# Pinning every engine's queue by the kernel's own list scheduler

## The chip, the cores and the metric

The kernel runs on one core of one Trainium2 chip. The metric is the device time of one execution in microseconds (us), lower is better; the median of several runs is compared. The core has five queues that work at the same time and each strictly in order: PE (TensorE, matmuls and their weight loads), DVE (VectorE), ACT (ScalarE), POOL (GpSimd) and SP, which here only issues DMA transfers. An instruction that must wait for data from another engine holds up everything behind it on its own queue.

## The reference

Three stages, one after the other, in fp32 accuracy:

```python
# 1. linear attention with a complex decay; B=2, H=8, S=768, D=48
S_re, S_im = a_t * (S_re, S_im) + (outer(k_t, v_t), 0)   # for every step t
y_t = q_t @ S_re
# 2. x is y as 1536 x 384;  w_in 384 x 2048, w_out 2048 x 384
x = softplus(x @ w_in) @ w_out
# 3. four experts;  w1 384 x 1024, w2 1024 x 384 each, p the normalised domain_probs
out = sum(p[:, e:e+1] * (relu(x @ w1[e]) @ w2[e]) for e in range(4))
```

## The kernel before, in words

The 768 steps of each of the two batch entries are cut into chunks of 128. Two chunks form a pair, so there are six pairs, n = 0 to 5, each with the chunks c = 0 and 1. For a pair, DVE and ACT turn the factors a into logarithm and angle (`t`, `im`, `re`), PE makes their running sums by a matmul with a triangle (`pf` for the angle, `pl` for the logarithm, L592), a row of carry goes from chunk to chunk by a small DMA (`rows`) and a POOL addition (L573), and DVE multiplies the results with q and k into `QK` (L664). PE then transposes `QK` (`tp`, L673; ACT copies it to `qT` and `kT`), multiplies it to `sp` (L682), DVE masks that to `A` (L683), and PE makes the chunk's output `yps` (L698) and its state `sps` (L709). ACT and DVE write the output as a high and a low half of fp32r into `X` (L720, L721).

The two feed-forward stages are cut into twelve steps k: k = 0, 1 and 6, 7 are the softplus layer of batch 0 and 1 in halves of the hidden width, the others are the experts. They run in this order:

```python
ORDER = (0, 1, 2, 3, 6, 7, 4, 5, 8, 9, 10, 11)
```

For a block of tokens and 128 hidden columns, a step does a first product `h` (L233, nine matmuls: three pieces of the depth by three products of high and low halves), an activation on ACT (`e`, L248 and L103; then DVE, L251), the split into `g` high and low (L276 and L277, or L286 and L287), and the second product `y` or `z` (L315). Step 0 works in blocks of 256 tokens, two chunks, so its first product needs `X` of both chunks of pair 0. The weights of the softplus layer come as 64-bit words (`rawA`, `rawB`); DVE joins the two words in three instructions (L70 to L72, to `fA`, `fB`), ACT and DVE split them (L182, L183), and SP writes the joined weights to DRAM for batch 1 (L201). The tile names are followed by step, weight piece and half.

All this is emitted from a list of events, each with a position; a stage spreads its units over a stretch of positions beside the feed-forward steps:

```python
def put(units, lo, hi):
    for i, u in enumerate(units):
        events.append((lo + (hi - lo) * i / len(units), len(events), u))
...
put(back(0), -7.9, -3.8)
...
put(back(1), -0.7, 6.3)
```

What is emitted in this order goes to the framework's own scheduler, which takes the order of emission as priority and decides, by its own durations, in which order each engine's queue stands. The kernel adds a few edges without a wait (`behind`), which only keep the loads of ACT's function tables and a pair of matmuls in place. At the end comes a test that the inputs are in the range for which this fast path holds; it doesn't matter here.

Of the kernel before, what the change touches and what calls it, by code (L numbers as in the profile page):

```python
# [10 lines left out]
F32R = mybir.dt.float32r  # L11
# [6 lines left out]
PSUM = bass.MemoryType.PSUM  # L18
ACT = mybir.EngineType.Activation
# [4 lines left out]
P = 128  # L24
# [30 lines left out]
TRIG = "trig_and_small"  # L55


def decode(nc, dst, raw, b_exp, pool):
    e = pool.tile([P, 768], I32, name="dec_e", bufs=1)
    hi_ = raw[:, :, 1]  # L60
    nc.vector.tensor_scalar(e, hi_, 20, 0x7FF, ALU.logical_shift_right, ALU.bitwise_and)
    nc.scalar.activation(e, e, AF.Relu, bias=b_exp, scale=float(2 ** 23))
    nc.vector.tensor_scalar(dst.bitcast(I32), hi_, 0x000FFFFF, 0x00100000, ALU.bitwise_and, ALU.bitwise_or)
    nc.vector.scalar_tensor_tensor(dst, raw[:, :, 0].bitcast(U32), 2.0 ** -32, dst.bitcast(I32), ALU.mult, ALU.add)
    nc.vector.scalar_tensor_tensor(e, hi_, -0x80000000, e, ALU.bitwise_and, ALU.bitwise_or)
    nc.vector.scalar_tensor_tensor(dst, dst, 2.0 ** -20, e.bitcast(F32), ALU.mult, ALU.mult)
# [9 lines left out]
def fast_path(ctx: ExitStack, tc, bad, wsc, qkv, a_re, a_im, w_in, w_out, probs, w1, w2, out):  # L76
    nc = tc.nc

    const = ctx.enter_context(tc.tile_pool(name="const", bufs=1))
    wp = ctx.enter_context(tc.tile_pool(name="wp", bufs=1))  # L80
    xa = ctx.enter_context(tc.tile_pool(name="xa", bufs=1))
    ac = ctx.enter_context(tc.tile_pool(name="ac", bufs=1))
    tmp = ctx.enter_context(tc.tile_pool(name="tmp", bufs=1))
    att_ctx = ExitStack()
    att = att_ctx.enter_context(tc.tile_pool(name="att", bufs=1))
    psum = ctx.enter_context(tc.tile_pool(name="psum", bufs=1, space=PSUM))
    early_ctx = ExitStack()
    early = early_ctx.enter_context(tc.tile_pool(name="early", bufs=1, side="right"))

    NOSYNC = mybir.DependencyInfo(mybir.DependencyClass.NoSync, mybir.DependencyReason.DATA)  # L90
    tabs = {"load": None, "since": []}

    def behind(ins, earlier):
        tc.add_manual_dep(ins.ins, earlier.ins.name, NOSYNC, reason="order on one engine")

    def use_table(name):
        load = nc.scalar.preload_act_table_set(name)  # L97
        for i in tabs["since"]:
            behind(load, i)
        tabs["load"], tabs["since"] = load, []  # L100

    def act(out_, in_, fn, **kw):
        i = nc.scalar.activation(out_, in_, fn, **kw)  # L103
        if fn in (AF.Exp, AF.Ln, AF.Sin, AF.Arctan):
            behind(i, tabs["load"])
            tabs["since"].append(i)
        return i
# [7 lines left out]
                            base=0, channel_multiplier=-1)  # L115
# [150 lines left out]
    def second(k, blk, f):  # L266
        if k % 6 >= 2:
            return
        key = (k, blk, f)
        if k == 0:  # L270
            if f % 2 == 0:
                return
            t = t_t.pop(key)
            hi, lo = (tmp.tile([P, 2, WM], F32R, tag="g", name=f"g{i}{k}_{blk}_{f}", bufs=GB).rearrange("p a b -> p (a b)")[:, :512]
                      for i in range(2))
            nc.scalar.copy(hi, t)  # L276
            nc.vector.tensor_tensor(lo, t, hi.bitcast(F32), ALU.subtract)  # L277
            for i in range(2):
                g_t[k, blk, f - 1 + i] = [x[:, i * 256:(i + 1) * 256] for x in (hi, lo)]
            if f == 1:  # L280
                low_sum(k, blk, hi[:, :256], 256)
            return
        t = t_t.pop(key)
        TB = span(k, blk)[-1]
        g = tmp.tile([P, 2, WM], F32R, tag="g", name=f"g{k}_{blk}_{f}", bufs=GB)[:, :, :TB]
        (nc.scalar.copy if k == 1 else nc.vector.tensor_copy)(g[:, 0, :], t)  # L286
        nc.vector.tensor_tensor(g[:, 1, :], t, g[:, 0, :].bitcast(F32), ALU.subtract)  # L287
        g_t[key] = g
        if k == 6 and f == 0:
            low_sum(k, blk, g[:, 0, :], TB)  # L290

    def third(k, blk, f):
# [15 lines left out]
        for j in range(nj):  # L308
            for n, (p, q) in enumerate(((0, 0), (0, 1), (1, 0))):
                if s < 2:  # L310
                    l_, r_ = wt[:, q, f % 2, j * P:(j + 1) * P], g[p] if k == 0 else g[:, p, :]
                else:
                    l_, r_ = g[:, p, j * P:(j + 1) * P], wt[:, q, f % 2, :]
                mate = k == 0 and j == 1
                mm = nc.tensor.matmul(ys[j], l_, r_, start=(opens and n == 0 and not mate),  # L315
                                      stop=(closes and n == 2), skip_group_check=k == 0)
                if opens and n == 0:
                    if mate:
                        behind(mm, opened)
                    opened = mm  # L320
# [55 lines left out]
    late = {}  # L376
# [139 lines left out]
    def flush():  # L516
        if len(pipe) > 0:
            second(*pipe[-1])
        while pipe:
            third(*pipe.pop(0))  # L520
# [242 lines left out]
    def run():  # L763
        for _, _, u in sorted(events, key=lambda e: e[:2]):
            u()
        events.clear()
# [5 lines left out]
    one = [slice(0, 1), slice(1, 2)]  # L772
# [26 lines left out]
    base = [0] + [24 + 16 * i for i in range(12)]  # L799
    ring = []  # L800
# [11 lines left out]
    for m, k in enumerate(ORDER):  # L812
        if k in FAST:
# [6 lines left out]
            for i in range(16):  # L820
                hh, r = divmod(i, 8)
# [6 lines left out]
            for n in range(8):  # L828
                j = n // 2
                if n % 2 == 0:  # L830
                    need, last = base[m] + 4 * j, base[m] + 4 * j + 4
                else:
                    need = base[m] + 8 * (j // 2) + 4 + 2 * (j % 2)
# [20 lines left out]
    for pos, need, last, k, n in sorted(fast_events):  # L854
# [3 lines left out]
        for i, u in enumerate(us):  # L858
            at = pos if i == 0 else max(pos + 2.5, need - 5.2 + 1.7 * (i - 1))
# [8 lines left out]

    def swap():
        early_ctx.close()  # L870
        xb = ctx.enter_context(tc.tile_pool(name="xb", bufs=1, side="right"))
        XB[1] = xb.tile([P, 2, KT, S], F32R, name="X1")

    put([swap], base[2] + 3.5, base[2] + 4)
# [2 lines left out]
    w_ = (b1 - b0) / 3  # L877
    for i, n in enumerate((3, 4, 5)):
        at = b0 + i * w_
# [4 lines left out]

    def switch():
        att_ctx.close()
        lp = ctx.enter_context(tc.tile_pool(name="late", bufs=1))
        for n in "xugwh":
            late[n] = lp
        home[1] = lp  # L890
# [50 lines left out]
    put(checks + [verdict], base[8] + 2, base[12] - 2)  # L941
    run()
    flush()


@with_exitstack
def general_path(ctx: ExitStack, tc, xs, v, qkv, a_re, a_im, w_in, w_out, probs, w1, w2, out):
# [80 lines left out]
    for t, src in zip(ws, (w_in, w_out)):  # L1028
        for j in range(8):
            raw = wk.tile([P, 768, 2], I32, name="graw", bufs=1)  # L1030
            nc.sync.dma_start(raw.rearrange("p a w -> p (a w)"), src.bitcast(I32)[j])
            decode(nc, t[:, j, :], raw, b_exp, wk)
# [65 lines left out]
@with_exitstack  # L1098
def attention_moe_kernel(ctx: ExitStack, tc, qkv, a_re, a_im, w_in, w_out, probs, w1, w2, v, out):
    nc = tc.nc  # L1100
    top = ctx.enter_context(tc.tile_pool(name="top", bufs=1))
    bad = top.tile([1, 1], I32, name="bad")
    wsc = nc.dram_tensor("moe1_weights", (16, P, 768), F32).ap()
    fast_path(tc, bad, wsc, qkv, a_re, a_im, w_in, w_out, probs, w1, w2, out)
    xs = nc.dram_tensor("attention_out", (NTOK, HD), F32).ap()
    flag = nc.values_load(bad[0:1, 0:1], min_val=0, max_val=1)
    with tc.If(flag > 0):
        general_path(tc, xs, v, qkv, a_re, a_im, w_in, w_out, probs, w1, w2, out)
# [53 lines left out]
```

## Time and profile before

| | before |
|---|---|
| time, median of 3 runs | 736.75 us (736.65 to 739.24) |
| the profiled execution | 736.14 us, of which the span from first to last instruction is 734.4 us |
| PE busy, share of the span | 699.3 us, 95% |
| DVE busy | 580.3 us, 79% |
| ACT busy | 488.2 us, 66% |
| granted TensorE clock, mean | 0.989 of full speed |

A matmul's records overlap, so "busy" is the time covered by at least one of them, and a PE that is busy need not be at its full rate. The shares are means over stages that differ: attention and the joining of weights load DVE and ACT in the first 140 us, after that the feed-forward steps alone set the load of PE.

### The profile page before, as it was taken

The page shows a single profiled execution, that of the slowest core. Times are in us where ns is not written, and L with a number is a line of the kernel's source. Part 1 is how long each engine was busy: PE and PEld are TensorE (multiplying, and loading weights), DVE is VectorE, ACT ScalarE, POOL GpSimd, SP SyncE. Part 2 cuts the span into 40 slices and gives each one's busy share as a digit, 9 for nine tenths or more (in the row PEclk, how much of TensorE's full clock was granted, in tenths as well). Part 3 has the DMA queues.
Part 4 walks back from the last instruction along what each step waited for, and adds up shares of the span by engine and source line. Part 5 has one row for each costly group of instructions (what it writes and reads, how often), then busy time and mean ns, then how long its engine had stood idle before and what let it go on. Part 6 is the DMA issues. An engine that isn't in the chain of part 4 may idle for free.

```text
span 734.4 us, 13295 instructions
## 1 busy us (share of the span) xinstructions
PE 699.3 (95%) x5171; PEld 674.2 (92%) x5171; DVE 580.3 (79%) x1139; ACT 488.2 (66%) x898; POOL 29.5 (4%) x29
## 2 busy tenths in 40 slices
PE   2778999999999999999999999999999999999997
PEld 1567898999899999999999999999999999999997
DVE  6899998945774863648888789988888898988963
ACT  8887885878995856345676666564556566666640
POOL 0112010000112011000000000000000000000000
PEclk9799999999999999999999999999999999999999
DMA  8666665721221330121022030213445445454512
GB/s 268 193 200 194 214 188 188 225 65 44 68 62 60 103 100 2 58 87 44 23 85 67 23 100 29 87 44 87 138 151 150 142 147 176 151 172 135 171 40 69
DMA packets 36486, 83.56 MB, mean 114 GB/s; under 512 B 4544, under 2 KB 13376, under 8 KB 36416
## 3 DMA queue, kind: packets, MB, share of 16 engines
q1 hardware_dynamic: 36128, 82.35, 36.3%
q8 instruction: 42, 0.69, 0.4%
q10 hardware_dynamic: 288, 0.30, 0.1%
q14 instruction: 28, 0.23, 0.1%
HBM read 73.95 MB, written 8.65 MB: 112 GB/s over the span
## 4 chain that ended last, share of the span: by engine, by line
PE 71%; ACT 12%; DVE 8%; DMA 6%; issue 2%; POOL 0%; SPq 0%; DVEq 0%; ACTq 0%; POOLq 0%
PE y L315 21%; PE h L233 16%; PE z L315 10%; PE px L426 8%; PE pv L426 4%; PE pc L426 2%; PE yps L698 2%; PE tp L673 2%; PE sp L682 2%; DMA chkw<-in_w_in_dram 2%; ACT L97 2%; ACT t L103 1%; ACT e L103 1%; DMA rawB<-in_w_dram 1%; PE ya L360 1%
## 5 line engine op out<-in xcount | busy, mean ns | idle before, releaser
L233 PE MATMUL h<-X,A 128*128 128x384 f32 (+1 forms) x936 | 174.9, 328 | 1.6 <-DVE e L251 0.9
L233 PEld LDWEIGHTS h<-X,A 128*128 128x128 f32 x936 | 152.6, 189 | 5.0 <-issue 1.8
L315 PE MATMUL y<-B,g 128*128 128x384 f32 x744 | 150.2, 335 | 0.2 <-DVE acc L346 0.2
L315 PEld LDWEIGHTS y<-B,g 128*128 128x128 f32 x744 | 131.1, 188 | 0.7 <-ACT he L446 0.5
L315 PE MATMUL y<-g,B 128*128 128x384 f32 (+1 forms) x504 | 90.3, 315 | 0.9 <-ACT g L286 0.3
L315 PE MATMUL z<-B,g 128*128 128x384 f32 x372 | 84.8, 335 | 0.0
L315 PEld LDWEIGHTS y<-g,B 128*128 128x128 f32 x504 | 78.9, 189 | 2.0 <-ACT g L286 0.7
L315 PEld LDWEIGHTS z<-B,g 128*128 128x128 f32 x372 | 66.5, 188 | 0.0
L248 ACT ACTIVATE e<-h 128x384 f32<-128x384 f32 (+1 forms) x60 | 30.7, 511 | 34.5 <-PE h L233 30.5
L251 DVE SCALAR_TENSOR_TENSOR e<-h,e 128x384 f32<-128x384 f32 (+1 forms) x60 | 34.8, 580 | 20.1 <-ACT e L103 19.1
L256 DVE SCALAR_TENSOR_TENSOR g<-h,g 128x384 fp32r<-128x384 f32 x32 | 17.7, 553 | 28.2 <-ACT g L255 28.2
L103 ACT ACTIVATE e<-e,b_one 128x384 f32<-128x384 f32 (+1 forms) x60 | 38.2, 637 | 1.4
L673 PE MATMUL tp<-ident,QK 128*96 128x128 f32 x192 | 27.1, 288 | 8.2 <-DVE QK L664 7.8
L673 PEld LDWEIGHTS tp<-ident,QK 128*96 128x96 f32 x192 | 22.3, 132 | 12.8 <-issue 4.9
L103 ACT ACTIVATE e<-e 128x384 f32<-128x384 f32 (+1 forms) x60 | 32.8, 546 | 1.2
L426 PE MATMUL px<-XC,sA 128*128 128x384 f32 x144 | 33.1, 338 | 0.5 <-DVE ha L452 0.5
L426 PE MATMUL px<-X,sA 128*128 128x384 f32 x144 | 33.3, 337 | 0.0
L315 PE MATMUL z<-g,B 128*128 128x384 f32 x144 | 33.3, 337 | 0.0
L287 DVE TENSOR_TENSOR g<-e,g 128x384 fp32r<-128x384 f32 x48 | 26.6, 554 | 6.1 <-ACT g L286 5.5
L255 ACT ACTIVATE g<-h 128x384 fp32r<-128x384 f32 x32 | 15.7, 489 | 21.9 <-PE h L233 21.7
L491 ACT CAST B<-rawB 128x768 fp32r<-128x768 f32 x24 | 20.0, 834 | 13.2 <-DMA rawB<-in_w_dram 6.2
L491 ACT CAST A<-rawA 128x384 fp32r<-128x384 f32 (+1 forms) x48 | 20.3, 457 | 11.7 <-DMA rawA<-in_w_dram 9.4
(204 smaller groups left out, 1409.3 us busy)
## 6 DMA issues: line engine op xcount, KB each, us to landing
rawA<-in_w_dram SPq DMA_DIRECT2D x32, 384.0 KB, 3.1
rawB<-in_w_dram SPq DMA_DIRECT2D x32, 384.0 KB, 3.1
rawA<-in_w_in_dram SPq DMA_DIRECT2D x16, 384.0 KB, 3.5
rawB<-in_w_out_dram SPq DMA_DIRECT2D x16, 384.0 KB, 3.4
chkw<-in_w_in_dram SPq DMA_DIRECT2D x16, 384.0 KB, 3.4
chkw<-in_w_out_dram SPq DMA_DIRECT2D x16, 384.0 KB, 3.3
qk<-in_qkv_dram SPq DMA_DIRECT2D x12, 384.0 KB, 3.2
v<-in_qkv_dram SPq DMA_DIRECT2D x12, 256.0 KB, 3.2
```

The lines of the kernel that those rows point to most:

```text
L97: load = nc.scalar.preload_act_table_set(name)
L103: i = nc.scalar.activation(out_, in_, fn, **kw)
L233: nc.tensor.matmul(ps, wt[:, p, kk, o:o + P], XB[b][:, q, kk, tok], start=(n == 0), stop=(n == 3 * KT - 1))
L248: nc.scalar.activation(t, h, AF.Abs)
L251: nc.vector.scalar_tensor_tensor(t, h, 0.0, t, ALU.max, ALU.add)
L255: nc.scalar.activation(g[:, 0, :], h, AF.Relu)
L256: nc.vector.scalar_tensor_tensor(g[:, 1, :], h, 0.0, g[:, 0, :].bitcast(F32), ALU.max, ALU.subtract)
L287: nc.vector.tensor_tensor(g[:, 1, :], t, g[:, 0, :].bitcast(F32), ALU.subtract)
L315: mm = nc.tensor.matmul(ys[j], l_, r_, start=(opens and n == 0 and not mate), stop=(closes and n == 2), skip_group_check=k == 0)
L426: nc.tensor.matmul(ps, lt[:, p, li, :], rhs, start=(start and n == 0), stop=(stop and n == 2), skip_group_check=True)
L491: nc.scalar.copy(hi, src)
L673: nc.tensor.transpose(tp[:96, hh, :], src[:, hf * 4 + hh, :], ident)
```

## The change: what it does

All tile pools are wrapped in a class that notes for each tile its ring of buffers. When everything is emitted, `arrange` takes all instructions of the program, works out who needs whom (overlapping areas, free buffers), groups consecutive PE instructions that write one PSUM tile into one job that nothing may enter, and schedules all engines together: the engine that can start soonest takes, among its jobs that are ready by then, the one emitted first. Durations are a table in `cost`. Every queue is then pinned in the order found, by edges without waits (`behind` of each instruction on the one ahead of it). No computation is added or removed, the positions of the events stay, and the waits between engines stay those that the data need. All lines of the old code stand 241 further down in the new one (L233 becomes L474). The core of the diff:

```diff
+class Queues:
...
+    def behind(self, ins, earlier):
+        info = mybir.DependencyInfo(mybir.DependencyClass.NoSync, mybir.DependencyReason.DATA)
+        self.tc.add_manual_dep(ins, earlier.name, info, reason="order on one engine")
...
+    def cost(self, i, e, ins, outs):
...
+        if kind == "InstDMACopy":
+            return (0.45 if out * outs[0].ap[0][1] > 7500 else 0.1), 0.0
...
+            if i.ins[0].dtype == F32R:
+                hold = max(0.109, out * 0.4375e-3 + 0.005)
...
+        if e == DVE:
+            wide = [ap for ap in ins if math.prod(c for _, c in ap.ap[1:]) > 1]
+            fast = kind in ("InstTensorScalarPtr", "InstTensorCopy") and len(wide) == 1 and not self.in_psum(wide[0])
+            t = n / (1.92e3 if fast else 0.96e3)
+            return t + 0.07, t + 0.15
+        if e == ACT:
+            t = n / 0.96e3 + (0.1 if any(ap.tensor.name.startswith("b_") for ap in ins) else 0.0)
+            return t + 0.02, t + (0.075 if any(map(self.in_psum, ins)) else 0.11)
+        if e == POOL:
+            return (1.05, 1.1) if outs[0].ap[0][1] == 1 else (0.2 + n * 2.3e-3, 0.25 + n * 2.3e-3)
...
+    def arrange(self):
...
+            out = touch[k][1][0].tensor.name if eng[k] == PE and touch[k][1] else None
+            if out is None:
+                job[k] = len(jobs)
+                jobs.append([k])
+            else:
+                if prev is None or prev[0] != out:
+                    prev = (out, len(jobs))
+                    jobs.append([])
+                job[k] = prev[1]
+                jobs[prev[1]].append(k)
...
+        while any(ready):
+            best = None
+            for e in range(5):
+                if ready[e]:
+                    soon = max(free[e], min(ready[e].values()))
+                    j = min(j for j, t in ready[e].items() if t <= soon)
+                    if best is None or soon < best[0]:
+                        best = (soon, e, j)
+            _, e, j = best
+            del ready[e][j]
+            for k in jobs[j]:
+                t = start[k] = max(free[e], from_when(k))
+                hold, seen_ = cost[k]
...
+                    slow = 1.9 if e == PE and 15 < t < 36 else 1.0
+                    hold, seen_at[k] = hold * slow, t + seen_ * slow
+                free[e] = t + hold
+                queue[e].append(k)
...
+        for q in queue:
+            for a, b in zip(q, q[1:]):
+                self.behind(todo[b], todo[a])
...
-    const = ctx.enter_context(tc.tile_pool(name="const", bufs=1))
+    queues = Queues(tc)
+    const = queues.pool(ctx, "const")
...
     run()
     flush()
+    queues.arrange()
```

How this moves instructions is seen at three places. The first is DVE's queue ahead of the first product: the row L721 of `yps_1` writes the last `X` that the first `h` needs. Before, it stands here:

```order
66 L600 SCALAR_TENSOR_TENSOR im_132<-im_132,pf_1_367 128x384
67 L72 SCALAR_TENSOR_TENSOR fA_1_1_514<-rawA_1_1_500,fA_1_1_514 128x384
68 L183 TENSOR_TENSOR A_1_497<-fA_1_0_502,A_1_497 128x384
69 L683 TENSOR_TENSOR A_1_0_372<-sp_1_0_373,tri 128x512
70 L70 TENSOR_SCALAR fB_1_0_553<-rawB_1_0_535 128x384
71 L683 TENSOR_TENSOR A_1_1_386<-sp_1_1_387,tri 128x512
72 L554 TENSOR_TENSOR re_481<-re_481,t_483 128x768
73 L183 TENSOR_TENSOR A_1_497<-fA_1_1_514,A_1_497 128x384
74 L555 SCALAR_TENSOR_TENSOR re_481<-re_481,t_483 128x768
75 L71 SCALAR_TENSOR_TENSOR fB_1_0_553<-rawB_1_0_535,fB_1_0_553 128x384
76 L721 TENSOR_TENSOR X_121<-yps_1_393,X_121 128x3x128
77 L715 TENSOR_TENSOR S_317<-sps_1_436,S_317 96x512
```

In the changed kernel the same place of DVE's queue reads:

```order
75 L841 SCALAR_TENSOR_TENSOR im_132<-im_132,pf_1_367 128x384
76 L312 SCALAR_TENSOR_TENSOR fB_1_0_553<-rawB_1_0_535,fB_1_0_553 128x384
77 L311 SCALAR_TENSOR_TENSOR fB_1_1_574<-rawB_1_1_537,fB_1_1_574 128x384
78 L924 TENSOR_TENSOR A_1_0_372<-sp_1_0_373,tri 128x512
79 L312 SCALAR_TENSOR_TENSOR fB_1_1_574<-rawB_1_1_537,fB_1_1_574 128x384
80 L924 TENSOR_TENSOR A_1_1_386<-sp_1_1_387,tri 128x512
81 L424 TENSOR_TENSOR B_1_534<-fB_1_0_553,B_1_534 128x384
82 L310 TENSOR_SCALAR fA_2_0_631<-rawA_2_0_617 128x384
83 L956 TENSOR_TENSOR S_317<-sps_1_436,S_317 96x512
84 L311 SCALAR_TENSOR_TENSOR fA_2_0_631<-rawA_2_0_617,fA_2_0_631 128x384
85 L312 SCALAR_TENSOR_TENSOR fA_2_0_631<-rawA_2_0_617,fA_2_0_631 128x384
86 L962 TENSOR_TENSOR X_121<-yps_1_393,X_121 128x3x128
```

`X` of `yps_1` has moved from row 76 to row 86: ten instructions that stood behind it stand ahead of it now, eight of them the joining and splitting of weights, the others the state `S` (L715) and one of the factors of pair 2 (L556). Nothing that stood ahead of it has gone behind it.

The second place is DVE's queue in step 0, block 1, where L251 makes `e_1_3` from the product `h_1_2`. Before:

```order
165 L664 TENSOR_TENSOR QK_1_1302<-qk_1_769,im_482 128x16x48
166 L70 TENSOR_SCALAR fA_1_0_1365<-rawA_1_0_1324 128x384
167 L70 TENSOR_SCALAR fA_1_1_1409<-rawA_1_1_1326 128x384
168 L71 SCALAR_TENSOR_TENSOR fA_1_0_1365<-rawA_1_0_1324,fA_1_0_1365 128x384
169 L721 TENSOR_TENSOR X_121<-yps_0_1190,X_121 128x3x128
170 L72 SCALAR_TENSOR_TENSOR fA_1_0_1365<-rawA_1_0_1324,fA_1_0_1365 128x384
171 L71 SCALAR_TENSOR_TENSOR fA_1_1_1409<-rawA_1_1_1326,fA_1_1_1409 128x384
172 L554 TENSOR_TENSOR re_2146<-re_2146,t_2148 128x768
173 L251 SCALAR_TENSOR_TENSOR e_1_3_1232<-h_1_2_1152,e_1_3_1232 128x512
```

After the change DVE's queue reads there:

```order
164 L924 TENSOR_TENSOR A_0_1_1183<-sp_0_1_1184,tri 128x512
165 L505 TENSOR_SCALAR stats<-stats 128x1
166 L492 SCALAR_TENSOR_TENSOR e_1_3_1232<-h_1_2_1152,e_1_3_1232 128x512
167 L310 TENSOR_SCALAR fA_1_0_1365<-rawA_1_0_1324 128x384
168 L310 TENSOR_SCALAR fA_1_1_1409<-rawA_1_1_1326 128x384
169 L311 SCALAR_TENSOR_TENSOR fA_1_0_1365<-rawA_1_0_1324,fA_1_0_1365 128x384
170 L311 SCALAR_TENSOR_TENSOR fA_1_1_1409<-rawA_1_1_1326,fA_1_1_1409 128x384
171 L518 TENSOR_TENSOR g_1_3_1286<-e_1_3_1232,g_1_3_1285 128x512
172 L312 SCALAR_TENSOR_TENSOR fA_1_0_1365<-rawA_1_0_1324,fA_1_0_1365 128x384
173 L962 TENSOR_TENSOR X_121<-yps_0_1190,X_121 128x3x128
```

Here the move goes the other way: seven instructions that stood ahead of `e_1_3` now stand behind it.

The third place is SP's queue of DMA issues near the start, where `rows` is the carry and `rawB_0_1` a half of the first weights of the second product. Before:

```order
13 L193 DMA rawB_0_0_470<-in_w_out_dram 128x768
14 L618 DMA rows_1_205<-zl_130 1x16x24
15 L193 DMA rawB_0_1_472<-in_w_out_dram 128x768
16 L538 DMA re_481<-in_a_re_dram 128x2x384
17 L539 DMA im_482<-in_a_im_dram 128x2x384
18 L147 DMA pr<-in_probs_dram 128x48
19 L201 DMA moe_weights<-fA_0_0_379 128x384
```

After, SP's queue reads:

```order
13 L434 DMA rawB_0_0_470<-in_w_out_dram 128x768
14 L434 DMA rawB_0_1_472<-in_w_out_dram 128x768
15 L388 DMA pr<-in_probs_dram 128x48
16 L779 DMA re_481<-in_a_re_dram 128x2x384
17 L442 DMA moe_weights<-fA_0_0_379 128x384
18 L434 DMA rawA_1_0_498<-in_w_in_dram 128x768
19 L442 DMA moe_weights<-fA_0_1_426 128x384
```

The carry row L618 has left row 14; it stands at row 25 now, behind its sister row L617. From step 1 on (row 260 of DVE's queue and behind) the two kernels have nearly the same order on every engine; what differs there are neighbours that change places, and PE jobs that are no longer cut in two.

## Rows read from the trace of the kernel before

**Rows 1.** Windows: busy us (count) of PE, PEld, DVE, ACT, POOL; clock, DMA share, GB/s.

```profile
9.00:20.00 11.00, 5.33 (x9) 2.84 (x10) 10.81 (x19) 10.03 (x18) 0.00 (x0) 0.79 0.86 307
20.00:40.00 20.00, 15.85 (x139) 10.83 (x139) 17.93 (x33) 17.47 (x31) 4.87 (x4) 0.77 0.65 204
40.00:60.00 20.00, 14.68 (x198) 12.64 (x196) 19.39 (x34) 18.58 (x32) 2.23 (x2) 1.00 0.52 155
60.00:140.00 80.00, 76.07 (x906) 71.29 (x906) 75.91 (x146) 60.61 (x112) 7.73 (x4) 1.00 0.66 206
140.00:360.00 220.00, 218.89 (x1808) 210.70 (x1807) 140.87 (x234) 152.62 (x266) 13.58 (x11) 1.00 0.22 65
360.00:729.00 369.00, 368.19 (x2119) 365.77 (x2117) 312.49 (x663) 223.21 (x434) 0.00 (x0) 1.00 0.35 108
```

**Rows 2.** Waits of PE, 8.94 to 140 us: total us, times, longest.

```profile
PE tp L673 <- DVE QK L664: 7.5, 3, 3.8
PE pf L592 <- ACT im L103: 5.7, 1, 5.7
PE pf L592 <- POOL im L573: 2.3, 2, 1.4
PE h L233 <- DVE e L251: 0.9, 1, 0.9
```

**Rows 3.** Timeline of DVE, 38 to 49 us: start, length, instruction.

```profile
38.65 0.35 DVE L70 TENSOR_SCALAR fA<-rawA 128x384 int32<-128x384 int32 x1
38.92 0.67 DVE L713 COPY S<-sps 96x512 f32<-96x512 f32 x1
...
41.38 0.54 DVE L72 SCALAR_TENSOR_TENSOR fA<-rawA,fA 128x384 int32<-128x384 int32 x1
41.85 0.54 DVE L183 TENSOR_TENSOR A<-fA,A 128x384 fp32r<-128x384 f32 x1
...
46.47 0.57 DVE L721 TENSOR_TENSOR X<-yps,X 128x384 fp32r<-128x384 f32 x1
46.94 0.70 DVE L715 TENSOR_TENSOR S<-sps,S 96x512 f32<-96x512 f32 x1
47.54 0.97 DVE L556 TENSOR_TENSOR im<-im,re 128x768 f32<-128x768 f32 x1
48.40 0.57 DVE L72 SCALAR_TENSOR_TENSOR fB<-rawB,fB 128x384 int32<-128x384 int32 x1
```

**Rows 4.** Timeline of PE, 47 to 55 us and 86 to 88 us; idle before in brackets.

```profile
47.10 4.09 PE L233 MATMUL h<-X,A 128*128 128x256 f32 x32 [0.47 <-DVE X L721]
54.98 1.49 PE L673 MATMUL tp<-ident,QK 128*96 128x128 f32 x12 [3.79 <-DVE QK L664]
...
86.05 1.24 PE L315 MATMUL y<-g,B 128*128 128x256 f32 x9
87.13 1.24 PE L233 MATMUL h<-X,A 128*128 128x256 f32 x9
```

**Rows 5.** Timeline of DVE, 98 to 104 us.

```profile
98.80 0.62 DVE L70 TENSOR_SCALAR fA<-rawA 128x384 int32<-128x384 int32 x2
99.34 0.55 DVE L71 SCALAR_TENSOR_TENSOR fA<-rawA,fA 128x384 int32<-128x384 int32 x1
...
100.42 1.58 DVE L72 SCALAR_TENSOR_TENSOR fA<-rawA,fA 128x384 int32<-128x384 int32 x1
...
103.27 0.68 DVE L251 SCALAR_TENSOR_TENSOR e<-h,e 128x512 f32<-128x512 f32 x1
```

**Rows 6.** Timeline of POOL, 60 to 130 us.

```profile
63.51 2.59 POOL L548 TENSOR_TENSOR t<-t,t 128x768 f32<-128x768 f32 x1 [6.27 <-ACT t L547]
...
98.53 3.06 POOL L548 TENSOR_TENSOR t<-t,t 128x768 f32<-128x768 f32 x1 [24.43 <-ACT t L547]
```

**Rows 7.** Timeline of SP, the DMA queue, 13 to 25 us.

```profile
13.60 0.63 SPq L618 DMA_DIRECT2D rows<-zl  x1
14.27 0.56 SPq L193 DMA_DIRECT2D rawB<-in_w_out_dram  x1
...
24.57 0.51 SPq L617 DMA_DIRECT2D rows<-tail  x1
```

More of the change, by code (lines that the diff above doesn't have):

```diff
@@ L55, with __init__, tile @@
 TRIG = "trig_and_small"
+ENGINES = {mybir.EngineType.PE: 0, mybir.EngineType.DVE: 1, mybir.EngineType.Activation: 2,
+           mybir.EngineType.Pool: 3, mybir.EngineType.SP: 4}
+PE, DVE, ACT, POOL, SP = range(5)
+class Pool:
+    def __init__(self, queues, pool, name, after):
+        self.queues, self.pool, self.name, self.after = queues, pool, name, after
+    def tile(self, shape, dtype, tag=None, name=None, bufs=1):
+        t = self.pool.tile(shape, dtype, tag=tag or name, name=name, bufs=bufs)
+        self.queues.home[t.name] = ((self.name, tag or name), bufs, self.after)
+        return t
@@ L77, in fast_path @@
     nc = tc.nc
-    const = ctx.enter_context(tc.tile_pool(name="const", bufs=1))
[L80 to L83, printed above, removed]
+    queues = Queues(tc)
+    const = queues.pool(ctx, "const")
+    wp = queues.pool(ctx, "wp")
+    xa = queues.pool(ctx, "xa")
+    ac = queues.pool(ctx, "ac")
+    tmp = queues.pool(ctx, "tmp")
     att_ctx = ExitStack()
-    att = att_ctx.enter_context(tc.tile_pool(name="att", bufs=1))
-    psum = ctx.enter_context(tc.tile_pool(name="psum", bufs=1, space=PSUM))
+    att = queues.pool(att_ctx, "att")
+    psum = queues.pool(ctx, "psum", space=PSUM)
     early_ctx = ExitStack()
-    early = early_ctx.enter_context(tc.tile_pool(name="early", bufs=1, side="right"))
-    NOSYNC = mybir.DependencyInfo(mybir.DependencyClass.NoSync, mybir.DependencyReason.DATA)
+    early = queues.pool(early_ctx, "early", side="right")
     tabs = {"load": None, "since": []}
     def behind(ins, earlier):
-        tc.add_manual_dep(ins.ins, earlier.ins.name, NOSYNC, reason="order on one engine")
+        queues.behind(ins.ins, earlier.ins)
+        queues.order_only.append((ins.ins.name, earlier.ins.name))
     def use_table(name):
@@ L870, in swap @@
         early_ctx.close()
-        xb = ctx.enter_context(tc.tile_pool(name="xb", bufs=1, side="right"))
+        xb = queues.pool(ctx, "xb", after="early", side="right")
         XB[1] = xb.tile([P, 2, KT, S], F32R, name="X1")
@@ L886, in switch @@
         att_ctx.close()
-        lp = ctx.enter_context(tc.tile_pool(name="late", bufs=1))
+        lp = queues.pool(ctx, "late", after="att")
         for n in "xugwh":
```

154 lines of the change are left out of this document (added).

## The prediction

> **What bounds the kernel now.** I read the windows first, since a share over the whole span mixes stages. PE idles 5.67 us of the 11 between 9 and 20 us, 4.15 between 20 and 40, 5.32 between 40 and 60, 3.93 between 60 and 140, 1.11 between 140 and 360, and 0.81 from there to 729 [rows 1]. So from 140 us on PE is full, and no order of the queues can give more than 1.92 us there; what can be won lies in the 19.07 us before. DVE, in the same windows, idles 2.07 us between 20 and 40, 0.61 between 40 and 60 and 4.09 between 60 and 140: 6.77 us of 120, it is the busiest engine until 60 us and level with PE until 140 [rows 1]. The waits of PE name the same thing: 7.5 us for `QK` from DVE, 5.7 for the arctangent on ACT right after the start, 2.3 for the carry that POOL adds, 0.9 for `e` from DVE [rows 2]. The granted clock is 0.77 to 0.79 between 9 and 40 us, where PE has only gapped work, and 1.00 behind that [rows 1]; PE waits there for others, so a faster or slower clock in that stretch is not priced.
>
> The profiled execution took 736.14 us (span 734.4), 0.6 below the median of the runs, 736.75. I make the sum against the former and add 0.6 at the end.
>
> **The change, part by part.** No instruction comes or goes, and edges without waits cost nothing by themselves: each is between two neighbours of one queue, which run in that order anyway. So PE's work is fixed, and the time moves by what its idle time gains or loses.
>
> *9 to 40 us.* The first 5.67 us wait for the first arctangent on ACT, whose chain from the first loads keeps its order. On SP the carry `rows<-zl`, which waits until 13.60, no longer holds up the weights behind it, issued at 14.27 [rows 7]; they can go right behind the issue before. But what PE waits for in this stretch is `QK` and the carry (L617, issued at 24.57), not these weights. I take 0; ends: 0.9 gained (the carry's shorter wait, 2.3 less 1.4 [rows 2]) and 0.5 lost (one more weight step of 0.47 us ahead of the first `QK`).
>
> *40 to 60 us: a loss.* `X` of `yps_1` gets ten DVE instructions more ahead of it. Start to start they cost: a join or split step 0.47 us (41.38 to 41.85), L70 0.27 (38.65 to 38.92), L715 0.60 (46.94 to 47.54), L556 0.86 (47.54 to 48.40) [rows 3]. Six steps, two L70, one L715 and one L556 are 2.82 + 0.54 + 0.60 + 0.86 = 4.8 us. By that alone the first `h` starts at 51.9 instead of 47.10 [rows 4], and PE has nothing else to do. But before the change PE idles again right behind it, 3.79 us, until `QK` of pair 1 lets the transposes start at 54.98 [rows 4]. Most of the ten stand ahead of that `QK` already; new ahead of it are only one split, one L70 and two join steps, 1.7 us. So the delay that is left at the transposes is 1.7 us, less what DVE's own idle shrinks until there. Of the 2.68 us of DVE idle between 20 and 60 [rows 1] I take a third, 0.9, since the new order chooses among ready work but can't make data come sooner. Loss: 0.8 us. Ends: a gain of 1.0 (all of the 2.68 gone) and a loss of 4.8 (nothing absorbed).
>
> *60 to 140 us: a gain.* Here the order moves the other way. `e_1_3` (103.27) loses seven instructions ahead of it, which took from 98.80 to 103.27, 4.5 us [rows 5]; by the same count `e_1_7` of step 0 loses five steps and one L70, 2.6 us, and `e_1_5`, between the two, 1.2 us. These instructions are the ones that feed PE; what is put behind them is weights that are wanted later. PE's visible idle in this window is 3.93 us [rows 1], of it the 0.9 for `e` and 1.4 for POOL's carry [rows 2], which also starts from DVE. The earlier DVE work exceeds most of these waits, so I take four fifths: 3.1 us. Ends: 0 and 3.9.
>
> *Inside the busy time.* Nine matmuls of 256 columns take 1.08 us start to start at best (86.05 to 87.13), 0.120 each; the 32 at 47.10 took 4.09, 0.128 each [rows 4]. Step 0 has three blocks of eight pieces with nine matmuls each for `h` and `y`, 432 in all; at 0.008 us each the small waits that no gap shows are at most 3.5 us. Jobs that are not cut and inputs that come earlier may close a part; I take 0.8. Ends: 0 and 3.5.
>
> *POOL beside DVE.* The list of durations has no price for DVE and POOL at once. In the trace, L72 took 1.58 us at 100.42, under POOL's addition of 3.06 us that began at 98.53, instead of 0.55, so 1.0 us lost [rows 5, 6]. The order decides which DVE instruction meets POOL, not whether one does: 0. [...] By rows the ends are a gain of 1.0 and a loss of 4.6 (5.65 us of POOL's own length [rows 6], less 1.0).
>
> *140 us to the end.* The orders agree but for neighbours; of 1.92 us idle nothing is promised to go: 0. Ends: 1.9 gained; 1.0 lost, if a transposition now kept behind a whole `h` job makes a chain late by one such job of nine 0.120 us matmuls [rows 4].
>
> Sum: + 0.8 - 3.1 - 0.8 = - 3.1 us; 736.14 - 3.1 = 733.0, and 733.6 for the median, rounded to 733.5.
>
> **The rivals.**
>
> *A larger gain.* DVE loses nearly all its idle and PE's gaps behind 20 us close. Adding the good ends, 0.9 + 1.0 + 3.9 + 3.5 + 1.9 = 11.2 us, gives 725.5; a likely value is three quarters, 728. For it: only weight work is moved, and DVE is loaded to 94% (113.2 of 120 us [rows 1]), so cover is always there. Against: the first 5.67 us and most of the 7.5 for `QK` are chains through several engines.
>
> *No change.* The loss ahead of the first `h` is 1.7 us, with none of DVE's idle won back, and the 60 to 140 gain is half, 2.0: 736.4. For it: the old order was also made by emission order and readiness, and behind step 0 most rows agree.
>
> *Slower.* The first `X` is late by 4.8 us, and PE doesn't get it back, because the waits behind it are not DVE's load but chains that begin with this `X` or with PE itself. With nothing won the time is 736.75 + 4.8 = 741.5. It decides from the point where the transposes of pair 1 start later than 54.98 by more than the 3.93 us that can be had behind 60.
>
> [...]
>
> **How the numbers follow.** About 0.5%, 3.7 us, is what a measurement of this kernel can tell from no change. My forecast, 731.5 to 735.5, has 0.43, a little over half of it below the line at 733.1: 0.22 faster, 0.21 same. The larger gain has 0.24, all faster. No change has 0.17, the port 0.04, both same. Slower has 0.12; 0.11 of it lies beyond the line at 740.4, 0.01 within. Together: faster 0.46, same 0.43, slower 0.11. The range goes from 726, near the sum of the good ends, to 740, into the slower case; it leaves out some 0.13.
>
> **What would show it.** In the trace after: the first long run of `h` starts 3 to 5 us later than 47.10, and the transposes behind it at 55 to 57. PE's idle between 60 and 140 is under 1.5 us. DVE's idle between 20 and 140 is under 6 us. From 140 on PE is as full as before. I am wrong if the transposes come later than 58, if PE's idle behind 60 stays at 4 us although `e` comes earlier, or if gaps on PE open behind 140 us, where the pinned queues can't step aside for a late transfer.

## The result, and the profile after

The changed kernel takes 730.9 us, median of 5 runs (728.62 to 732.11), against 736.75: the ratio of the mean times is 0.9903, 95% interval 0.9875 to 0.9932, so 5.0 to 9.2 us less. The forecast was 733.5, range 726 to 740: faster, as forecast, by about twice as much. The profiled execution took 730.9 us, span 729.1. A few executions of 785 us and more, of changed and unchanged kernels alike, are left out of all ratios here.

The windows of the changed kernel, columns as in [rows 1]:

```profile
9.00:20.00 11.00, 4.93 (x8) 2.27 (x8) 10.80 (x19) 9.57 (x17) 0.00 (x0) 0.78 0.79 291
20.00:40.00 20.00, 13.67 (x132) 9.32 (x130) 19.79 (x38) 18.99 (x33) 4.04 (x3) 0.78 0.82 264
40.00:60.00 20.00, 17.58 (x197) 15.25 (x198) 17.58 (x27) 15.90 (x29) 5.19 (x4) 0.83 0.41 129
60.00:140.00 80.00, 77.93 (x937) 74.92 (x937) 75.69 (x148) 63.18 (x118) 6.59 (x4) 1.00 0.64 199
140.00:360.00 220.00, 219.43 (x1816) 213.48 (x1816) 144.73 (x241) 153.12 (x268) 13.36 (x11) 1.00 0.21 66
360.00:724.00 364.00, 363.34 (x2086) 360.09 (x2085) 305.99 (x655) 219.09 (x429) 0.00 (x0) 1.00 0.35 109
```

PE's idle is the stretch less the first busy number. It grew between 20 and 40 us from 4.15 to 6.33, and fell from 5.32 to 2.42 between 40 and 60, from 3.93 to 2.07 between 60 and 140, and from 1.11 to 0.57 between 140 and 360; behind that it is 0.66. The weight loads (second number) say more than that: between 60 and 140 us they cover 74.92 us instead of 71.29, with 937 matmuls instead of 906. PE does more in the same window than its busy time shows. The granted clock differs too: 0.83 between 40 and 60 us, where it was 1.00 before [rows 1].

The waits of PE up to 140 us, in the changed kernel:

```profile
PE pf L833 <- ACT im L344: 6.1, 1, 6.1
PE tp L914 <- DVE QK L905: 3.0, 1, 3.0
PE tp L914 <- ACT qT L915: 2.2, 1, 2.2
PE h L474 <- DVE e L492: 1.8, 1, 1.8
PE tp L914 <- ACT kT L915: 1.3, 1, 1.3
PE pl L833 <- POOL t L814: 1.0, 2, 0.8
```

Against [rows 2]: the waits for `QK` fell from 7.5 us to 3.0, those for POOL's carry from 2.3 to 1.0. The wait for `e` grew from 0.9 to 1.8. The transposes now wait 2.2 and 1.3 us for the copies `qT` and `kT` on ACT; before it was 0.2 for `qT`.

The timeline of PE at the first `h`, in the changed kernel, answers to [rows 4]:

```profile
43.01 1.65 PE L833 MATMUL pl<-t,tri 128*128 128x384 f32 x2 [0.75 <-POOL t L814]
44.45 3.62 PE L923 MATMUL sp<-qT,kT 96*128 96x128 f32 x16
...
52.10 0.50 PE L474 MATMUL h<-X,A 128*128 128x256 f32 x2 [0.61 <-ACT X L961]
52.96 4.33 PE L474 MATMUL h<-X,A 128*128 128x256 f32 x34 [0.36 <-DVE X L962]
57.13 1.91 PE L914 MATMUL tp<-ident,QK 128*96 128x128 f32 x16
```

The long run of `h` starts 5.9 us later than 47.10, but the transposes behind it only 2.15 later than 54.98, and with no wait. The product `sp` ahead of it was late already; in the kernel before it stands here:

```profile
40.45 2.29 PE L682 MATMUL sp<-qT,kT 96*128 96x128 f32 x16
```

Up to the transposes PE runs the same 312 matmuls in both kernels, and from there to the fifth `h` job of step 1 (at 148.05 and 143.98 us) again the same work, all but a few matmuls that overlap the edges. These stretches compare better than windows at fixed times; columns as in [rows 1], first the kernel before, then the changed one:

```profile
0.00:54.98 54.98, 31.68 (x312) 22.85 (x313) 45.59 (x88) 46.91 (x78) 7.20 (x13) 0.88 0.69 221
54.98:148.05 93.07, 88.02 (x984) 82.07 (x984) 88.19 (x168) 73.50 (x140) 8.72 (x5) 1.00 0.65 201
0.00:57.13 57.13, 34.33 (x312) 24.88 (x313) 48.19 (x93) 48.19 (x81) 9.18 (x14) 0.82 0.68 223
57.13:143.98 86.85, 84.78 (x986) 81.63 (x984) 82.23 (x160) 69.46 (x133) 7.73 (x5) 1.00 0.63 197
```

In the first stretch PE idles no longer than before (22.80 us against 23.30), but the same matmuls take 2.65 us more, at a lower granted clock (0.82 against 0.88). The second stretch, with a granted clock of 1.00 in both, is 6.2 us shorter: 3.0 us of idle are gone (5.05 to 2.07), and 3.2 us of busy time.

DVE in step 0, block 1, in the changed kernel, answers to [rows 5]:

```profile
98.45 0.68 DVE L492 SCALAR_TENSOR_TENSOR e<-h,e 128x512 f32<-128x512 f32 x1
99.04 0.64 DVE L310 TENSOR_SCALAR fA<-rawA 128x384 int32<-128x384 int32 x2
```

`e_1_3` runs at 98.45 instead of 103.27, 4.8 us earlier, and the joins stand behind it.

### The profile page after: what moved, and what is told of

It reads as the page before. It is cut to its first block, busy times and chain, and to the rows that moved or that the text cites. A ratio compares the mean times of both kernels' runs of the same rounds, so it can differ in the third digit from the quotient of the medians.

```text
span 729.1 us, 13309 instructions
## 1 busy us (share of the span) xinstructions
PE 698.0 (96%) x5171; PEld 676.1 (93%) x5171; DVE 577.9 (79%) x1139; ACT 485.9 (67%) x898; POOL 30.3 (4%) x29
## 3 DMA queue, kind: packets, MB, share of 16 engines
HBM read 73.95 MB, written 8.65 MB: 113 GB/s over the span
## 4 chain that ended last, share of the span: by engine, by line
PE 83%; DVE 8%; ACT 1%; issue 1%; DMA 1%; DVEq 0%
PE y L556 26%; PE h L474 19%; PE z L556 11%; PE px L667 9%; PE pv L667 4%; PE sp L923 3%; PE pc L667 3%; PE yps L939 2%; PE tp L914 2%; PE sps L950 1%; DVE acc L587 1%; PE ya L601 1%; DVE g L678 1%; DMA rawA<-in_w_dram 1%; ACT L338 1%
## 5 line engine op out<-in xcount | busy, mean ns | idle before, releaser
L474 PE MATMUL h<-X,A 128*128 128x384 f32 (+1 forms) x936 | 169.7, 326 | 2.7 <-DVE e L492 1.8
L474 PEld LDWEIGHTS h<-X,A 128*128 128x128 f32 x936 | 152.0, 189 | 4.5 <-DVE e L492 2.0
L556 PE MATMUL y<-B,g 128*128 128x384 f32 x744 | 150.7, 337 | 0.6 <-DVE Y L573 0.2
L556 PEld LDWEIGHTS y<-B,g 128*128 128x128 f32 x744 | 130.7, 188 | 2.5 <-DVE acc L587 1.5
L556 PE MATMUL y<-g,B 128*128 128x384 f32 (+1 forms) x504 | 88.6, 316 | 0.4 <-ACT g L527 0.3
L556 PE MATMUL z<-B,g 128*128 128x384 f32 x372 | 84.7, 335 | 0.0
L556 PEld LDWEIGHTS y<-g,B 128*128 128x128 f32 x504 | 78.1, 189 | 1.7 <-ACT g L527 0.7
L556 PEld LDWEIGHTS z<-B,g 128*128 128x128 f32 x372 | 66.4, 188 | 0.0
L587 DVE SCALAR_TENSOR_TENSOR acc<-y,pr,acc 128x384 f32<-128x384 f32 x46 | 27.0, 611 | 15.2 <-PE y L556 15.1
L556 PE MATMUL z<-g,B 128*128 128x384 f32 x144 | 32.8, 336 | 0.0
L923 PEld LDWEIGHTS sp<-qT,kT 96*128 96x128 f32 x192 | 25.4, 203 | 1.0 <-DVE fB L310 0.3
```

What stands on the lines that cost most here:

```text
L474: nc.tensor.matmul(ps, wt[:, p, kk, o:o + P], XB[b][:, q, kk, tok], start=(n == 0), stop=(n == 3 * KT - 1))
L587: nc.vector.scalar_tensor_tensor(dst, ys[j], pcol, dst, ALU.mult, ALU.add)
L923: nc.tensor.matmul(sp[:, hh, :], kT[:, hh, :], qT[:, hh, :], start=True, stop=True)
```

## The experiments

Twelve kernels, in three lots; each ratio is to the kernel before on the same chip, with its 95% interval. The first lot splits the pinning by time and by engine. In `early_only` and `late_only` the pins end or begin at the fifth `h` job of step 1:

```diff
+        T = min(start[k] for k in range(N) for ap in touch[k][1] if ap.tensor.name.startswith("h1_0_4"))
         for q in queue:
             for a, b in zip(q, q[1:]):
-                self.behind(todo[b], todo[a])
+                if start[b] < T:          # late_only: start[b] >= T
+                    self.behind(todo[b], todo[a])
```

> Only what the list scheduler starts before the fifth h job of step 1 (PE: h1_0_4, 144 us in the trace after) is pinned; behind that the framework's own order stands, as before. Theory A (the gain is made by the order of the first 144 us, where PE still waits): 4.1 us below before, the lead that the trace after shows at that job, about 732.6. Theory B (the gain is made in the long stage in which PE is full, because its jobs are no longer cut): within 1.5 us of before, 735.3 or more.

Measured: 0.9938 (0.9920 to 0.9957), 4.6 us below before.

> The other half: the framework's order as before up to h1_0_4, the list scheduler's order pinned from there on. Theory A: only the 1.6 us by which the lead grows between 190 and 300 us in the trace after, about 735.1. Theory B: 4 us or more below before, 732.7 or less.

Measured: 0.9977 (0.9960 to 0.9995), 1.7 us below before. The two halves together give 0.9915, the whole gave 0.9903: within the intervals the parts add up, and theory A's split holds.

What the late half does can be read. Waits of PE's weight loads between 140 and 360 us, with `early_only`, where the late order is that of before:

```profile
PEld pl L828 <- ACT hl L826: 1.4, 6, 0.3
...
PEld tp L916 <- DVE QK L907: 0.6, 1, 0.6
PEld pf L828 <- ACT hl L822: 0.5, 1, 0.5
```

The waits for these tiles are in no line of `late_only`'s list for that stretch, which begins:

```profile
PEld sps L952 <- issue: 1.3, 5, 0.3
PEld yps L941 <- issue: 1.2, 5, 0.2
PEld h L476 <- issue: 0.8, 4, 0.2
```

The running sums `pl` and `pf` used to enter PE's queue before ACT had written their input `hl`, and stood between pieces of an `h`; now they stand behind whole jobs, when `hl` is there. That is 1.9 us of waits gone, and 0.6 for a `tp`. Some small waits are new (all that are listed come to 6.9 us with `early_only` and 5.6 with `late_only`); 1.7 us were measured, 0.4 to 2.9 by the interval.

The other two of this lot pin one queue:

```diff
-        for q in queue:
+        for q in (queue[PE],):            # dve_only: (queue[DVE],)
```

> Only PE's queue is pinned, in the order of the changed kernel with its uncut jobs; DVE, ACT, POOL and SP are left to the framework's scheduler (which orders them around the pinned PE). Theory A (DVE's order gives the gain, PE only follows): no gain behind 60 us, within 1.5 us of before, 735.3 to 738. Theory B (PE's own order gives it): 731 to 733.

Measured: 1.0037 (1.0022 to 1.0051), slower than before.

> Only DVE's queue is pinned in the order of the changed kernel, the four others are the framework's. Theory A: most of the lead up to 144 us is there, 2.5 to 4 us below before, 732.7 to 734.3. Theory B: within 1.5 us of before.

Measured: 1.0148 (1.0127 to 1.0169), 11 us slower. This contradicts theory A as I had put it: DVE's order alone doesn't carry the gain, it costs. Neither theory had that.

The second lot frees one queue of the five, or changes the carry or the jobs.

```diff
-        for q in queue:
+        for q in (queue[PE], queue[DVE], queue[ACT], queue[POOL]):   # all_but_sp
+        for q in (queue[DVE], queue[ACT], queue[POOL], queue[SP]):   # all_but_pe
+        for q in (queue[PE], queue[ACT], queue[POOL], queue[SP]):    # all_but_dve
```

> The changed kernel, but SP's queue is not pinned; the framework's scheduler orders it around the four pinned queues, and puts the carry of pair 1 (rows<-tail) ahead of the write and the load of weights that stand before it in the changed kernel. Theory C (the first h is late by 5 to 6 us because of the carries' place on SP): the first h at 47 to 50 us instead of 52.1, and a time 1 to 2 us below the changed kernel, 729 to 730. Theory D (it is late because ten more DVE instructions stand ahead of X): the first h within 0.7 us of 52.1, and the time of the changed kernel, 730 to 732.

Measured: 0.9921 (0.9899 to 0.9942), as the changed kernel. Its traced execution took 736.49 us, 4.5 above the median of its runs, so the trace speaks for the order and not for the time. In it the first two `h` came at 49.90, 2.2 us earlier than in the changed kernel, but the rest at 52.80, for DVE's `X`: DVE stood idle for 1.78 us, without a cause that the profile shows, ahead of one of the ten instructions that the new order puts before `X` (L310, at 50.26). SP's order is not where the gain is; between C and D this run leaves it open.

> The changed kernel, but PE's queue is left to the framework, around the four pinned queues. Theory A in its first form (DVE's order makes the gain, PE only follows): within 2 us of the changed kernel, 730 to 733. Theory E (what counts is that all queues are ordered by one schedule; one queue ordered by other durations waits for the rest): slower than before, 738 to 748, as with DVE alone pinned.

Measured: 1.0080 (1.0057 to 1.0103). With DVE, ACT, POOL and SP ordered exactly as in the changed kernel, PE in the framework's order makes it slower than before. Theory E holds, the first form of A falls. Windows of `all_but_pe`:

```profile
60.00:140.00 80.00, 74.98 (x884) 68.31 (x883) 68.69 (x132) 55.07 (x103) 6.78 (x4) 1.00 0.57 177
```

Not only PE, DVE and ACT too do less than before in this window (68.69 and 55.07 us busy, against 75.91 and 60.61 in [rows 1]). ACT's largest wait there is for PE's `h`, first with `all_but_pe`, then in the changed kernel:

```profile
ACT e L489 <- PE h L474: 18.5, 6, 4.3
ACT e L489 <- PE h L474: 9.3, 7, 2.7
```

So ACT's pinned queue stands twice as long at an `e` for which PE has not yet made the `h`.

`carry_on_act` issues the carry from ACT's queue:

```diff
-        nc.sync.dma_start(rows[0][0:1, 0, :], tail[127:128, :])
-        nc.sync.dma_start(rows[0][0:1, 1, :], dlam[127:128, :])
+        nc.scalar.dma_start(rows[0][0:1, 0, :], tail[127:128, :])
+        nc.scalar.dma_start(rows[0][0:1, 1, :], dlam[127:128, :])
```

> The changed kernel, with the two small carry transfers issued from ACT's queue, right behind the instructions that make them, so that no weight transfer stands ahead of them; the list scheduler then orders everything anew. Theory C: POOL's carry additions come 1.5 to 3 us earlier than at 28.75 and 38.33, the first h at 47 to 50, the time 1 to 3 us below the changed kernel, 728 to 730. Theory D: the first h stays at 51 to 53, the time within 1 us of the changed kernel.

Measured: 0.9923 (0.9910 to 0.9937), as the changed kernel. It didn't test what it should: the first two issues took 0.63 and 0.59 us and left ACT idle for 0.79, as its timeline shows (ACTq is ACT's own issuing):

```profile
25.87 0.63 ACTq L858 DMA_DIRECT2D rows<-tail  x1
26.54 0.59 ACTq L859 DMA_DIRECT2D rows<-zl  x1
27.18 0.61 ACT L344 ACTIVATE re<-re,b_hpi 128x384 f32<-128x384 f32 x1 [0.79 <-ACT re L875]
```

and POOL's additions came at 29.77 and 39.85, later than 28.75 and 38.33. But it shows something else. The first `h` was at 53.45 and the transposes at 59.84, 2.7 us later than in the changed kernel, and still the fifth `h` job of step 1 started at 143.78, against 143.98, and the time is the same. Most of the 2.7 us came from idle that PE no longer had:

```profile
60.00:140.00 80.00, 80.00 (x962) 77.59 (x961) 75.75 (x148) 64.59 (x122) 6.34 (x4) 1.00 0.61 192
```

`cut_jobs` lets the scheduler put other work between the matmuls of one tile:

```diff
-                if prev is None or prev[0] != out:
+                if True:                                                   # cut_jobs
+                if prev is None or prev[0] != out or out.startswith("h"):      # cut_h
+                if prev is None or prev[0] != out or not out.startswith("h"):  # cut_all_but_h
```

> The changed kernel, but every PE instruction is a job of its own, so that the list scheduler may cut the runs of matmuls that write one tile, as the framework's did. Theory A (the early gain is DVE's and PE's common order, the uncut jobs give the 1.6 us between 190 and 300): the lead at 144 us stays at 3 to 4.5, the late 1.6 us are gone, 732 to 733. Rival: uncut jobs don't matter, the lead at 300 us is 5 to 6, 730 to 732.

Measured: 0.9974 (0.9960 to 0.9989), 1.9 us below before: three quarters of the gain are gone, more than either side expected. In its window the weight loads show it:

```profile
60.00:140.00 80.00, 78.14 (x921) 72.94 (x915) 73.85 (x139) 62.01 (x114) 7.31 (x5) 1.00 0.59 184
```

PE idles no more than in the changed kernel (1.86 us against 2.07), but the weight loads cover 72.94 us instead of 74.92. In DVE's queue the sixth `e` of step 0, which is `e_1_3` in the two kernels, came about as late as before (103.27 [rows 5]) and not as early as in the changed kernel (98.45):

```profile
104.36 0.67 DVE L492 SCALAR_TENSOR_TENSOR e<-h,e 128x512 f32<-128x512 f32 x1
```

The third lot asks which jobs must stay whole, and whether DVE's order is needed when the rest is pinned.

> The changed kernel, but only the first products (tiles h) may be cut; all other PE jobs stay whole. Theory F (cutting costs because a cut first product delivers e late to ACT and DVE, which is what the first 144 us wait for): the gain is lost as with all jobs cut, 734.5 to 736.5. Rival G (cutting the other jobs, the second products and the small attention matmuls, costs): as the changed kernel, 730 to 732.5.

Measured: 0.9912 (0.9885 to 0.9940).

> The complement: the first products stay whole, all other PE jobs may be cut. Theory F: as the changed kernel, 730 to 732.5. Rival G: 734.5 to 736.5. If both this and the run before lie between, both kinds of jobs count.

Measured: 0.9921 (0.9904 to 0.9938). Both have the gain of the changed kernel. So F falls and G too: no one kind of job explains the loss of `cut_jobs`. Cutting both kinds gives another schedule for all engines (in the traces DVE's order differs from the changed kernel's in 300 of 1139 places), and which of its differences costs the time is open; the late `e` is one candidate.

> The changed kernel, but DVE's queue is left to the framework, around the four pinned ones. Theory A (the order of DVE's work, with the joining of weights behind what feeds PE, is needed for the gain): 735 or more. Rival (PE's uncut jobs with ACT's order are enough, DVE's order follows anyway): 730 to 733.

Measured: 1.0053 (1.0036 to 1.0070), slower than before. With the four other orders as they are, DVE's is needed for the gain, as PE's is; the rival falls. ACT and POOL were not freed in any run.

`nudged` gives 14 jobs another place in the order of priority:

```diff
-                    j = min(j for j, t in ready[e].items() if t <= soon)
+                    j = min((j for j, t in ready[e].items() if t <= soon), key=lambda j: j + NUDGE.get(j, 0))
...
+NUDGE = {74: 76, 94: -63, 96: -55, 119: 162, 171: 559, 181: 28, 197: -354, 304: 385, 324: 693, 348: -55,
+         395: 124, 456: -80, 597: 272, 808: 377}
```

> The changed kernel with other priorities for 14 of its jobs in the first 140 us; above all the copies qT and kT of the first chunk now stand ahead of ACT's logarithm of pair 1, which held PE up for 2.24 us at 29.3 us in the trace after. Theory H (what the first 60 us lose is still lost at the end, because PE is full behind them): 1.5 to 3.5 us below the changed kernel, 727.5 to 729.5. Rival I (the first 60 us have slack, as the carry from ACT's queue indicated: 4.9 us late at the transposes of pair 1, 4.3 us early at 148): within 1 us of the changed kernel.

Measured: 0.9873 (0.9853 to 0.9893), median 728.47 us, the fastest of all. It is 2.4 us below the changed kernel's median, though the kernel before stood at 738.12 us beside it and at 736.75 beside the changed kernel; the two intervals overlap by 0.0018, so that it beats before is shown, that it beats the change is likely. The size is as H had it, but not for H's reason: priorities were changed in all of the first 140 us, and it is not the 20 to 60 us that gained. The wait for `qT` did shrink from 2.2 to 0.9, and a wait of 2.5 for POOL's carry took its place; waits of PE between 18 and 140 us:

```profile
PE tp L918 <- DVE QK L909: 3.1, 1, 3.1
PE pf L837 <- POOL im L818: 2.8, 2, 2.5
...
PE tp L918 <- ACT qT L919: 0.9, 1, 0.9
```

PE's idle between 20 and 60 us is 8.65 us, as in the changed kernel (8.75). Behind that it idles less, 0.58 us up to 140 instead of 2.07:

```profile
20.00:40.00 20.00, 15.08 (x136) 10.22 (x135) 19.92 (x40) 18.90 (x32) 2.60 (x2) 0.76 0.82 260
40.00:60.00 20.00, 16.27 (x189) 13.73 (x187) 15.77 (x24) 15.34 (x27) 5.80 (x4) 0.83 0.45 140
60.00:140.00 80.00, 79.42 (x946) 76.22 (x946) 76.15 (x149) 63.88 (x119) 5.85 (x4) 1.00 0.64 197
```

But the traced execution took 730.18 us, 1.7 above the median, and in it the fifth `h` job of step 1 starts at 144.12, no earlier than the 143.98 of the changed kernel. Where the 2.4 us come from is not shown.

## Why the prediction came out as it did

The direction was right: PE nearly full behind 140 us, the gain mostly in the stage ahead of it, and a loss at the first `h` that the gain behind it outweighs. Of the signs, the transposes came at 57.13 (55 to 57 given); the run of `h` came 5.9 us later (3 to 5), PE's idle between 60 and 140 is 2.07 us (under 1.5), and DVE's idle between 20 and 140 is 6.94 us (under 6; it was 6.77 before). So DVE did not fill its idle time, as the forecast took it to; the gain came from what it does first. By the steps, measured at the same work in both kernels:

*9 to 40 us, taken as 0.* It lost 0.9 us, beyond the end of 0.5: behind the same matmuls, the transposes near its end start at 38.22 instead of 37.33. PE's idle in the two windows grew by 0.4 and 2.2, but its first matmul came earlier, at 7.98 instead of 8.94. The wait that shows is that for `qT` on ACT. ACT's queue has a table load of 1.28 us and a logarithm of pair 1 of 0.94 ahead of it in both kernels (`qT` at 28.67, before at 28.90). What changed is that PE had a running sum `pf` to do meanwhile, and now has not: POOL's carry addition, which `pf` needs, came at 28.75 instead of 26.96. I had the carry's wait as a possible gain, and it came later.

*40 to 60 us, a loss of 0.8.* From those transposes to the ones of pair 1 another 1.2 us were lost, close to the forecast; but the way there was not the one that I priced, and the near hit is in part luck. POOL's two carry additions ahead of it, first before, then in the changed kernel:

```profile
35.63 1.00 POOL L573 TENSOR_TENSOR t<-rows,t 1x384 f32<-1x384 f32 x1 [3.27 <-DMA rows<-t]
36.60 1.70 POOL L573 TENSOR_TENSOR im<-rows,im 1x384 f32<-1x384 f32 x1
...
38.33 2.96 POOL L814 TENSOR_TENSOR im<-rows,im 1x384 f32<-1x384 f32 x1 [5.25 <-DMA rows<-tail]
41.26 1.70 POOL L814 TENSOR_TENSOR t<-rows,t 1x384 f32<-1x384 f32 x1
```

They ended at 42.96 instead of 38.30, PE's `pl` waited for them, and `sp` behind it started at 44.45 instead of 40.45, 4.0 us late. Then `sp` took 3.62 us instead of 2.29: the granted clock was 0.50 between 44 and 48 us, and 1.00 in the kernel before; what lowered it is not shown. DVE waited for it, in the changed kernel:

```profile
46.40 0.69 DVE L924 TENSOR_TENSOR A<-sp,tri 128x512 f32<-128x512 f32 x1 [1.36 <-PE sp L923]
48.11 0.69 DVE L924 TENSOR_TENSOR A<-sp,tri 128x512 f32<-128x512 f32 x1 [0.55 <-PE sp L923]
52.35 0.55 DVE L962 TENSOR_TENSOR X<-yps,X 128x384 fp32r<-128x384 f32 x1
```

Before, the second `A` stood at 43.20 and this `X` at 46.47 (for `X` [rows 3]). So 4.9 of the 5.9 us were there at `A`, and between `A` and `X` DVE's order added 1.0. What the ten instructions cost by themselves is not shown, since DVE did part of them while it would have waited. Where the low clock falls is not set by the order alone: `early_only` has the same order up to 144 us, its clock was 1.00 between 44 and 48 and 0.50 between 52 and 54, and its long run of `h` started at 50.98, 3.9 us later than before. I had left the clock unpriced. That a late `h` is taken up by the wait behind it, and that most of the ten stand ahead of `QK` anyway, is right: the last `QK` started at 55.13 instead of 53.88.

*60 to 140 us, a gain of 3.1, and 0.8 inside the busy time.* `e_1_3` came 4.8 us earlier, 4.5 forecast. The fifth `h` job of step 1 starts at 143.98 us in PE's timeline of the changed kernel:

```profile
143.98 1.75 PE L474 MATMUL h<-X,A 128*128 128x384 f32 x9
```

and at 148.05 in that of before:

```profile
148.05 1.75 PE L233 MATMUL h<-X,A 128*128 128x384 f32 x9
```

From 2.15 us late at the transposes to 4.07 early here, the stretch gave 6.2 us. Of these 3.0 are idle, as forecast; by what the fixed window shows it is 1.9, since the rest lies between 55 and 60 and behind 140. The waits for `QK` and for the carry are gone from it, that for `e` is not. The other 3.2 us lie inside the busy time: the term that I sized too small, 0.8, though still under its end of 3.5. A busy PE hid waits, and the weight loads' share is the row that would have shown it: 71.29 of 80 us, against 210.70 of 220 and 365.77 of 369 where PE is full [rows 1].

*140 us on, taken as 0, ends 1.9 gained.* It gave 1.7 us, measured apart by `late_only`: near the end that I thought nothing promised. PE's visible idle between 140 and 360 fell by 0.54 only, so here too most of it was hidden, and idle time was no bound for what an order can give. The term that I gave as a risk (a chain kept behind a whole `h`) was the gain: what stands behind the whole job finds its input ready.

The steps come to 2.15 lost, 3.0, 3.2 and 1.7 gained, 5.8 us together, as much as the medians differ (5.85). What doubled the forecast are the hidden waits and the late stage.

*POOL beside DVE, 0.* On DVE's side the 0 is borne out at the carry: beside POOL's additions a factor and a join step took 1.28 and 1.34 us in the changed kernel, 1.24 and 1.35 before, where 0.94 and 0.54 are usual. But I looked at DVE alone. POOL's own addition took 2.96 us at 38.33 (3.42 in `early_only`, which has the same order), and 0.99 at 48.46, and PE waited for it. What makes it long is not shown.

Of the rivals, the slower case did not come. No run shows the loss of up to 4.6 us of DVE's time beside POOL for which the chances, as the port, have 0.04: in the changed kernel the longest DVE step beside POOL's addition of 2.79 us at 100.60 took 1.12 us, where 0.55 is usual. The larger gain put a likely value at 728; the changed kernel lies between it and my forecast, `nudged` reaches it.

What I argued and the runs took back: that DVE's order makes the gain and PE follows. Pinning DVE alone costs 1.5%, PE alone 0.4%; freeing either from the full set costs 1.8% and 1.5% against the changed kernel (PE 1.0080, DVE 1.0053, over 0.9903). What is shown is that the gain needs the orders of PE and DVE from one schedule, and that neither works with the framework's order around it. Which of the moves in 60 to 140 us are worth what isn't settled.

## What to carry to other kernels

When queues are pinned, pin all the engines that feed each other, from one schedule; here one pinned queue among others ordered by other durations was worse than none (1.0037 with PE's alone, 1.0148 with DVE's). Look at the weight loads' busy time beside the matmuls' to see waits that a busy PE hides (71.29 us beside 76.07 before, 74.92 beside 77.93 after, between 60 and 140 us), and don't take PE's idle time for the most that an order can give. Price a move by what it does to the stage in which PE last waits: transposes that came 2.7 us later in `carry_on_act` were made up for by 144 us. Before a late landmark is put down to the move, compare the granted clock and the waits ahead of it: at the first `h` they account for most of the delay (4.9 of the 5.9 us were there at `A`). 14 changed priorities perhaps took another 2.4 us off the median; that they beat the change is likely, not shown.
